# Attention and a highway layer on one core: the highway bias spread by a matrix product, in a new order of instructions

## The chip, the cores and the metric

The kernel runs on one core of a Trainium2 chip. A core has four computing engines that each run their own queue of instructions in order: PE (TensorE, matrix products, with its weight loads shown as PEld), DVE (VectorE), ACT (ScalarE) and POOL (GpSimd). A fifth queue, SP (SyncE), only issues transfers here. Engines wait for each other and for transfers by semaphores. The metric is the device time of one launch in microseconds (us); lower is better.

## What is computed

The reference first normalises queries and keys, attends, and then runs a highway layer on the heads side by side. Cut to what matters:

```python
q_n = q / (norm(q) + 1e-6);  k_n = k / (norm(k) + 1e-6)      # q, k, v: 8 x 12 x 448 x 64
scores = q_n @ k_n^T / tau                                   # tau = 0.1
attn = softmax(scores);  a = attn @ v
x = a.transpose(0, 2, 1, 3).reshape(3584, 768)
H = max(x @ w_h, 0)                                          # 768 x 768
T = sigmoid(x @ w_t + b_t)
out = T * H + (1 - T) * x
```

The change concerns b_t, the bias of the gate T, a vector of 768 numbers.

## The kernel before, in words

Work is cut into 8 batches, each of 6 pairs of heads (48 pairs, numbered s = 0 to 47), and 4 row groups of the highway layer for each batch (32 groups, g = 0 to 31). A batch has 448 rows; the first 384 lie in 3 blocks of 128 lanes, the other 64 are "tails", which two heads share.

Loading: POOL issues the large loads of q, k and v (tiles qr, kr, vr, 576 KB each, lines 342 and 365) and the two weights (wt, wh, line 372); SP issues the tails (qt, kt, vt, lines 357 to 367). All of these convert or keep the input's numbers and share the same transfer engines.

Normalising: squares (line 264 on ACT, line 258 on DVE or POOL; tile sq), folded sums (tile f, lines 421 and 425; n, line 427), a reciprocal root by Newton steps on DVE (tile rs, lines 465 to 471), and then q and k scaled into tile qn and, for the tails, kb (line 258).

Turning: for batches 0 to 3, PE turns qn and kb (lines 582, 585, 607) and DVE or ACT copies them out of PSUM (line 261). For batches 4 to 7, SP issues transposing transfers instead: qT from qn (line 572), tT from kb (line 599). The highway input xT comes from x by such transfers for batches 1 to 6 (line 757).

Attention for a pair: PE forms three blocks of scores into a ring of three PSUM tiles pS (line 642) and a block for the tail keys into a ring of two tiles pB (line 657); ACT takes the exponentials into E and Et (lines 648 and 661); PE multiplies them with the values in vp into pB again (lines 690, 694 and 710); DVE takes a reciprocal (line 718) and scales the result into x (line 720), which frees pB.

The highway group: PE multiplies xT with wt and wh into pS (lines 807, 791 for the tail groups, 779 for the last half group). ACT takes a tanh of the T half (lines 845 to 849), DVE combines (lines 867, 872, 879), DVE or POOL adds x (line 884), SP stores. For groups g below 24, b_t enters by one more matrix product of a row of ones with the bias row (tiles ones and bth). From g = 24 on (ADDED = 24), DVE adds it from tile bias instead, in which all 128 lanes hold the whole of b_t (lines 837 and 839). The two bth rows sit at lane 0 and lane 64, all other lanes of bth are zero.

PE runs its products in three forms, which the kernel calls T (two halves of 64 lanes side by side: lines 642 and 807), C (two halves of 64 columns: line 791) and F (the whole array: everything else).

The order of all of this is a table of numbers, ORDER, one number for each operation; SLOTS gives the buffer that each new tile takes in its ring; MOVED names the operations that run on their second choice of engine; URGENT lets a DVE operation wait for a POOL operation that came before it in the table. Nothing is scheduled at run time: each engine's queue is the table, filtered by engine. In the head, 40 products of the constant tile fill (line 310) keep PE running while it has nothing else.

Of the kernel before, what the change touches and what calls it, by code (L numbers as in the profile page):

```python
# [105 lines left out]
    int(n)  # L106
    for n in """
91 117 155 156 194 226 270 311 319 337 338 356 357 376 474 484 518 525 601 621 681 733 752 790 827 873 898 1059
1073 1088 1138 1175 1259 1288 1298 1338 1339 1374 1411 1428 1491 1502 1579 1596 1597 1614 1615 1617 1665 1682
""".split()  # L110
)

# [897 lines left out]
```

## Time and profile before

| What | us |
|---|---|
| Runs shown, median (lowest to highest), 3 runs | 269.06 (268.74 to 270.12) |
| Profiled execution, its span | 270.4 |
| PE busy, of that span | 244.4 |
| DVE busy | 228.5 |
| ACT busy | 206.0 |
| POOL busy | 115.9 |
| First scores of the first pair start on PE | 17.53 |
| The last product ends on PE, about | 264.4 |

For the profiled execution the span is the time on record: from its first instruction to its last. A row of the timeline has the start, the duration, the engine, the line, what is written and what is read, how often in a row, and in square brackets how long the engine was idle just before and what ended that. A row "xN" spans N instructions that follow each other. PE's busy time includes the filling and emptying of its pipeline, so a full slice does not say that PE is at its peak.

### The profile page before, as it was taken

How to read it: one execution, taken by the hardware profiler on the slowest of the kernel's cores; microseconds unless marked ns; L12 is line 12 of the kernel's file. 1: busy time of each engine (PE TensorE's matmuls, PEld its weight loads, DVE VectorE, ACT ScalarE, POOL GpSimd, SP SyncE). 2: the span in 40 equal slices, each digit the busy share in tenths (PEclk: the TensorE clock that was granted, in tenths of full speed). 3: DMA queues.
4: the chain of work that ended last, by engine and by line, in shares of the span. 5: the costliest groups of instructions: out<-in, count | busy, mean ns of one | idle time of the engine just before them, and what ended most of it. 6: DMA issues, size and time to landing. Idle time of an engine off the chain costs nothing.

```text
span 270.4 us, 9033 instructions
## 1 busy us (share of the span) xinstructions
PE 244.4 (90%) x3755; PEld 165.0 (61%) x3755; DVE 228.5 (85%) x513; ACT 206.0 (76%) x279; POOL 115.9 (43%) x151
## 2 busy tenths in 40 slices
PE   7088978999999999999899799997999999999991
PEld 3044666676776676667466557664767667767650
DVE  6599899999999898998976978997987864569894
ACT  3379999799999989989589499867868797961120
POOL 8757458563455649335450626314404522002140
PEclk9659999999999999999999799999999999999998
DMA  7999999999899797999999976999939949413133
GB/s 136 207 192 183 179 200 211 194 184 193 136 136 252 103 152 84 172 253 157 178 166 173 187 196 128 206 136 154 235 107 175 183 72 238 80 58 119 63 100 132
DMA packets 104025, 43.32 MB, mean 160 GB/s; under 512 B 97584, under 2 KB 101040, under 8 KB 103984
## 3 DMA queue, kind: packets, MB, share of 16 engines
q0 software_dynamic: 38608, 16.52, 49.1%
q1 hardware_dynamic: 63920, 25.50, 48.8%
q10 hardware_dynamic: 1456, 0.72, 1.0%
q8 instruction: 29, 0.48, 0.7%
q14 instruction: 12, 0.10, 0.1%
HBM read 38.21 MB, written 11.01 MB: 182 GB/s over the span
## 4 chain that ended last, share of the span: by engine, by line
PE 62%; DVE 20%; DMA 7%; issue 4%; ACT 3%; POOL 2%; SPq 1%; DVEq 0%; PEldq 0%; ACTq 0%; POOLq 0%
PE pS L807 26%; PE pS L642 9%; PE pB L694 8%; PE pS L791 4%; PE pB L710 4%; PE pB L657 3%; PE pB L690 3%; DMA kt<-in_k_dram 3%; DVE qn L258 3%; PE pB L582 2%; DMA qr<-in_q_dram 2%; DVE x L720 2%; DMA qT<-qn 2%; DVE f L421 2%; DVE hm L867 1%
## 5 line engine op out<-in xcount | busy, mean ns | idle before, releaser
L648 ACT ACTIVATE E<-pS 128x896 f16<-128x896 f32 x144 | 127.3, 924 | 26.2 <-PE pS L642 22.5
L807 PEld LDWEIGHTS <-xT 64*128 64x128 f16 x1128 | 53.8, 94 | 31.6 <-issue 2.6
L807 PE MATMUL pS<-wt,xT 64*128 64x384 f16 x576 | 56.6, 325 | 0.2 <-PEq L800 0.2
L807 PE MATMUL pS<-wh,xT 64*128 64x384 f16 x552 | 55.7, 323 | 0.2 <-DVE hm L867 0.2
L642 PE MATMUL pS<-qT 64*128 64x384 f16 x288 | 43.9, 332 | 2.3 <-DMA qT<-qn 1.8
L694 PE MATMUL pB<-vp,E 128*128 128x65 f16 x864 | 43.8, 194 | 0.0
L694 PEld LDWEIGHTS <-E 128*128 128x128 f16 x864 | 38.8, 98 | 2.6 <-issue 2.5
L867 DVE SCALAR_TENSOR_TENSOR hm<-pS,x 128x768 f16<-128x768 f32 (+1 forms) x33 | 27.3, 831 | 10.7 <-ACT tt L848 5.7
L642 PEld LDWEIGHTS <-qT 64*128 64x128 f16 x576 | 22.9, 95 | 19.6 <-issue 4.4
L690 PE MATMUL pB<-vp,Et 128*128 128x130 f16 x144 | 32.0, 222 | 2.3 <-DVE x L720 1.9
L258 POOL TENSOR_TENSOR qn<-kr,rs 128x384 f16<-128x384 f16 x24 | 19.8, 827 | 32.9 <-issue 10.0
L884 POOL TENSOR_TENSOR os<-x,hm 128x768 f32<-128x768 f16 (+1 forms) x11 | 15.8, 1441 | 37.7 <-DVE hm L879 17.3
L720 DVE SCALAR_TENSOR_TENSOR x<-pB,rd 128x448 f16<-128x448 f32 x48 | 29.7, 621 | 1.1
L661 ACT ACTIVATE Et<-pB 128x512 f16<-128x512 f32 x48 | 28.9, 609 | 0.9 <-PE pB L657 0.8
L642 PE MATMUL pS<-tT,qT 64*128 64x64 f16 x282 | 27.6, 190 | 0.0
L258 POOL TENSOR_TENSOR qn<-qr,rs 128x384 f16<-128x384 f16 x17 | 14.4, 850 | 14.0 <-DMA qT<-qn 5.6
L884 DVE TENSOR_TENSOR os<-x,hm 128x768 f32<-128x768 f16 (+1 forms) x22 | 18.5, 842 | 0.8 <-POOL os L884 0.6
L845 ACT ACTIVATE tt<-os 128x768 f16<-128x768 f32 (+1 forms) x8 | 6.1, 764 | 17.1 <-DVE os L839 10.0
L710 PE MATMUL pB<-vp,E 128*128 128x65 f16 x288 | 18.6, 195 | 0.5 <-POOL vp L261 0.5
L258 DVE TENSOR_TENSOR qn<-qr,rs 128x384 f16<-128x384 f16 x30 | 17.2, 577 | 0.5 <-POOL qn L258 0.4
L690 PEld LDWEIGHTS <-Et 128*128 128x128 f16 x144 | 14.1, 98 | 5.5 <-issue 4.3
L879 DVE TENSOR_TENSOR hm<-tt,hm 128x768 f16<-128x768 f16 (+1 forms) x33 | 16.4, 503 | 0.4
(116 smaller groups left out, 451.2 us busy)
## 6 DMA issues: line engine op xcount, KB each, us to landing
out_dram<-os SPq DMA_DIRECT2D x23, 384.0 KB, 3.0
vr<-in_v_dram POOLq DMA_DIRECT2D x8, 576.0 KB, 11.3
kr<-in_k_dram POOLq DMA_DIRECT2D x7, 576.0 KB, 10.8
qr<-in_q_dram POOLq DMA_DIRECT2D x7, 576.0 KB, 10.7
qt<-in_q_dram SPq DMA_DIRECT2D x16, 96.0 KB, 5.4
vt<-in_v_dram SPq DMA_DIRECT2D x16, 96.0 KB, 5.6
out_dram<-os SPq DMA_DIRECT2D x15, 96.0 KB, 2.7
kt<-in_k_dram SPq DMA_DIRECT2D x14, 96.0 KB, 6.7
```

What stands on the lines that cost most here:

```text
L258: return (nc.vector if eng == "DVE" else nc.gpsimd).tensor_mul(out_, a, c)
L642: ins = nc.tensor.matmul(dst, lhsT=qT[ln, 384 + 128 * c : 512 + 128 * c], rhs=rhs, start=True, stop=True)
L648: return nc.scalar.activation(R("E", s)[:, c, :, 0:448], R("S", 3 * s + c)[:, :, 0:448], AF.Exp, scale=inv_tau)
L661: op("ACT", f"expt {s}", lambda: nc.scalar.activation(R("Et", s)[:, 64:576], R("B", ("S", s))[:, :], AF.Exp, scale=inv_tau), key + 3, r=[( ...
L690: nc.tensor.matmul(U[:, 2 * c : 2 * c + 2, :].rearrange("p g e -> p (g e)"), lhsT=Et[:, 128 + 128 * c : 256 + 128 * c], rhs=vp[:, 6:8, :]. ...
L694: ins = nc.tensor.matmul(U[:, 2 * c + ab, :], lhsT=EF[:, j, 576 * ab + 128 * c : 576 * ab + 128 * c + 128], rhs=vp[:, 3 * ab + j, :], star ...
L710: ins = nc.tensor.matmul(U[:, 6, :], lhsT=lt, rhs=rh, start=(n == 0), stop=(n == 7))
L720: op("DVE", f"ev {s}", lambda: nc.vector.scalar_tensor_tensor(out=R("x", b)[:, :, D * p : D * p + D], in0=U_()[:, :, 0:D], scalar=0.0, in1 ...
L807: ins = nc.tensor.matmul(P[:, h, 0:MH], lhsT=lt, rhs=rh, start=(part == 0 and cc == (-1 if wi == 0 and not added else 0)), stop=(part == 1 ...
L867: return nc.vector.scalar_tensor_tensor(out=o_, in0=i0, scalar=0.0, in1=xs, op0=ALU.max, op1=ALU.subtract)
L879: op("DVE", f"gg{'h' if tail or last_ else ''} {nm}", lambda cs=cs: nc.vector.tensor_mul(R("hm", g)[:, cs], R("tt", g)[:, cs], R("hm", g)[ ...
L884: op(en, f"out{'h' if tail or last_ else ''} {nm}", lambda eng=eng, cs=cs: eng.tensor_add(R("os", g)[:, cs], xall()[:, cs], R("hm", g)[:, ...
```

## The change

Three things change. First, the transfer that spread b_t from memory over 128 lanes into tile bias goes. In its place PE multiplies a block of ones with the two bth rows, which leaves b_t in every lane of one pS tile, and DVE copies that to bias. Second, all four tables are new: ORDER, SLOTS, URGENT and MOVED. Third, by MOVED, some operations are on other engines: of the scaled q (qn from qr) DVE has 20 instead of 30 and POOL 27 instead of 17; of the last additions over 768 columns DVE has 11 instead of 15 and POOL 12 instead of 8; of the copies of v, DVE has 23 instead of 19, ACT 11 instead of 10 and POOL 14 instead of 19. All sizes, ring depths and the other operations stay.

```diff
-        op("POOL", "ld bb", lambda: nc.gpsimd.dma_start(bias[:, :], moe_b_t.partition_broadcast(128)), key + 30, w=[("bias", 0)])
+
+        def spread():
+            for h in range(2):
+                ln = slice(64 * h, 64 * h + 64)
+                ins = nc.tensor.matmul(R("S", ("bb", 0))[:, h, 0:MH], lhsT=ones[ln, 0:128], rhs=bth[ln, MH * h : MH * h + MH],
+                                       start=True, stop=True)
+            return ins
+
+        op("PE", "bbm", spread, key + 30, mode="T", r=[("zb", 0), ("bth", 0)], w=[("S", ("bb", 0))])
+        eng = pick("DVE", "ACT")
+        op(eng, "bbc", lambda eng=eng: copied(eng, bias.rearrange("p (h m) -> p h m", h=2), R("S", ("bb", 0))[:, :, 0:MH]), key + 30,
+           r=[("S", ("bb", 0))], w=[("bias", 0)])
...
-18 17 2 3 5 0 78 20 19 33 83 21 6 23 11 4 84 24 29 22 77 1 16 8 74 87 28 75 42 25 36 81 40 9 43 27 26 35 32 44
+0 28 16 3 8 39 29 18 17 12 2 43 87 79 90 9 15 27 21 1 20 40 24 26 44 25 31 33 14 73 32 85 19 22 77 23 36 5 6 45
```

The table's rows tell a reader nothing, so here is what stands in the queues at three places. Line numbers of the changed kernel are 1 lower up to line 376 and 10 higher from line 387 on.

The first place is POOL's queue where the three large loads of the last batch (7) are issued. Before, behind the fold of tile f, all three (qr, vr, kr) stand in a row:

```order
L425 TENSOR_TENSOR f_94<-f_92 128x192
L342 DMA qr_71<-in_q_dram 128x12x192
L365 DMA vr_83<-in_v_dram 128x12x192
L342 DMA kr_74<-in_k_dram 128x12x192
L258 TENSOR_TENSOR kb_81<-kt_79,rs_100 64x6x64 x2
```

In the changed kernel, POOL's queue at the same place, the loads of batch 7 from kr to vr:

```order
L435 TENSOR_TENSOR f_95<-f_93 128x192
L341 DMA kr_75<-in_k_dram 128x12x192
L260 COPY vp_87<-vr_82 128x6x64
L257 TENSOR_TENSOR qn_102<-qr_72,rs_98 128x2x3x64
L260 CAST vp_88<-vt_86 64x6x64
L341 DMA qr_72<-in_q_dram 128x12x192
L260 COPY vp_87<-vr_82 128x6x64
L364 DMA vr_83<-in_v_dram 128x12x192
```

Four operations of POOL now stand between the first and the last of the three loads.

The second place is SP's queue near there, where the key tails of batch 6 (the two loads into a kt tile) are issued. Before, both stand behind the first xT transpose of batch 3 (into xT_120) and behind two qT transposes:

```order
L757 DMA_TRANSPOSE xT_120<-x_116 128x12x128
L572 DMA_TRANSPOSE qT_106<-qn_102 128x6x128 x2
L891 DMA out_dram<-os_129 64x384
L361 DMA kt_78<-in_k_dram 64x6x64 x2
L757 DMA_TRANSPOSE xT_119<-x_116 128x9x128
```

In the changed kernel the same stretch of SP's queue; the tile of batch 6 is kt_79, and the xT transpose of batch 3 is into xT_119:

```order
L360 DMA kt_79<-in_k_dram 64x6x64
L908 DMA out_dram<-os_127 128x768
L582 DMA_TRANSPOSE qT_106<-qn_101 128x6x128
L356 DMA qt_77<-in_q_dram 64x6x64
L901 DMA out_dram<-os_130 64x384
L356 DMA qt_77<-in_q_dram 64x6x64
L767 DMA_TRANSPOSE xT_119<-x_116 128x12x128
L901 DMA out_dram<-os_130 64x384
L360 DMA kt_79<-in_k_dram 64x6x64
L582 DMA_TRANSPOSE qT_107<-qn_102 128x6x128
```

One of the two loads has moved ahead of that xT transpose, and the other has moved ahead of the two qT transposes behind it (the first of them is the last row). The square that reads these key tails has moved too: it stood in DVE's queue, and now stands in ACT's, between an exponential of a pair of batch 4 and the next.

The third place is the head. In the changed kernel's queue on PE, the new product (line 380) stands behind the last of the first 26 products of fill and in front of the turning of the first pair:

```order
L309 MATMUL pB_134<-fill 128x384
L380 LDWEIGHTS ones
L380 MATMUL pS_131<-bth,ones 128x384
L592 LDWEIGHTS qn_102
L592 MATMUL pB_134<-ident,qn_102 128x128
```

And on DVE, in the changed kernel, the copy to bias follows the copy of the first pair's turned rows (qT_107) and precedes the scaling of the next pairs:

```order
L260 COPY qT_107<-pB_134 128x896
L260 CAST bias<-pS_131 128x768
L257 TENSOR_TENSOR kb_80<-kt_79,rs_100 64x6x64
L257 TENSOR_TENSOR kb_80<-qt_77,rs_100 128x2x3x64
L257 TENSOR_TENSOR qn_101<-qr_70,rs_100 128x2x3x64
```

Before, nothing stood at either of these two spots; the transfer into bias was issued by POOL in the second half of the run. Counted over PE's whole queue, the three forms of product follow each other 135 times in a change of form before, and 162 times now: the parts of the highway products are cut finer between the scores and the products with the values.

More of the change, by code (lines that the diff above doesn't have):

```diff
@@ L93 @@
     for n in """
-001000101001011010001001001101200002010102110111002010110010120120101112011200001100210200010111101211100200011
-010121101110012010001110200001001021200211101012020101011010201110110121100211010001102011120112012121110000101
-100021101121211010022102010100101020101012011210211201110120121001020201210110020012110220201001111102111010011
-012001102000110023200021110200121101110010012110121010210102210000201001000112011010203210111001102010110021110
-201210221101220100000001111210001102221120101021010210121001021011001110121001110123101211022001101020020100112
-201101000120122101120201010102001010110220011012020001102010211111010202120100211120011122111012120012100110211
-000200021110010011001010202112221011000010120001001101210001101010221101220201130110201020012020011110100221020
-21032102101100121011102301000121210121010230201
+111001101012110000001000222020002201001101101000101101121100000012210010101110220010101211001010111101121100010
+001200110101201001001000121100112112200221101000010012101012001011001121001021201000211221110012001102001110001
+201110110011222002010002011101101112000101201012100001121111001210110010102220110222110211100010022110010111101
+210010021012023110001021100112120101002200020011210211001002000110111011021110210021122301101012101031212101111
+111010110010220201012102011011021222101110001210221031122201101121110120021021001120100101121010221020121010201
+110201211001000101222000010222102011202011201000110111110020021110021011110200111210011112210012211000100102321
+020120002010101001022010012100201011211111201112001102002010102002120021211100002011102101311102101202200100111
+002210202011102201100101230112011200212210002110
 """.replace("\n", "")
@@ L107 @@
     for n in """
-91 117 155 156 194 226 270 311 319 337 338 356 357 376 474 484 518 525 601 621 681 733 752 790 827 873 898 1059
-1073 1088 1138 1175 1259 1288 1298 1338 1339 1374 1411 1428 1491 1502 1579 1596 1597 1614 1615 1617 1665 1682
+94 195 227 271 312 339 342 357 446 475 505 524 525 587 918 958 976 994 996 1011 1119 1137 1139 1193 1196 1212
+1339 1360 1375 1376 1393 1394 1396 1411 1429 1461 1476 1492 1538 1579 1580 1597
 """.split()
```

147 rows, old and new, of tables (MOVED, ORDER) are left out of this document.

## The prediction

> **What bounds the kernel now.** I read the page first, then a table of stages, then the timeline wherever PE stood still. The page:
>
> ```profile
> span 270.4 us, 9033 instructions
> PE 244.4 (90%) x3755; PEld 165.0 (61%) x3755; DVE 228.5 (85%) x513; ACT 206.0 (76%) x279; POOL 115.9 (43%) x151
> ```
>
> PE leads, but DVE and ACT are near. The stages tell them apart (columns: window, its length, busy time and instructions of PE, PEld, DVE, ACT, POOL, then PE's clock, the transfer engines' share, GB/s):
>
> ```profile
> 17.50:50.00 32.50, 27.54 (x431) 18.88 (x431) 30.91 (x69) 31.06 (x43) 19.34 (x30) 0.98 1.37 193
> 50.00:130.00 80.00, 79.35 (x1312) 55.46 (x1310) 74.65 (x171) 73.59 (x99) 42.54 (x50) 1.00 1.17 167
> 147.00:156.00 9.00, 7.11 (x109) 4.92 (x107) 8.90 (x21) 5.19 (x7) 4.40 (x6) 0.81 1.35 180
> ...
> 186.00:190.00 4.00, 2.24 (x46) 1.51 (x41) 2.77 (x5) 2.77 (x5) 1.60 (x2) 1.00 1.13 251
> 190.00:250.00 60.00, 59.98 (x980) 41.71 (x979) 44.45 (x97) 43.87 (x59) 13.62 (x17) 1.00 0.66 138
> ```
>
> Up to 50 us DVE and ACT are full (30.91 and 31.06 of 32.50) and PE waits for them. From 50 us on PE hardly ever rests, so whatever is added to PE's own queue there lengthens the run, and whatever shortens DVE alone does not. What can be won behind 50 us are the few places where PE does stand still. The two largest:
>
> ```profile
> 136.29 1.09 POOL L342 DMA_DIRECT2D qr<-in_q_dram  x1
> ...
> 138.37 1.03 POOL L342 DMA_DIRECT2D kr<-in_k_dram  x1
> 137.63 2.21 SPq L361 DMA_DIRECT2D kt<-in_k_dram  x2
> 138.36 8.51 DMA kt<-in_k_dram
> 146.96 0.56 DVE L258 TENSOR_TENSOR sq<-kt 128x384 f16<-128x384 f32 x1 [2.31 <-DMA kt<-in_k_dram]
> 148.70 0.19 PE L657 MATMUL pB<-tT 128*128 128x64 f16 x1
> 150.78 0.22 PE L690 MATMUL pB<-vp,Et 128*128 128x130 f16 x1 [1.89 <-DVE x L720]
> 152.00:154.00 2.00, 2.00 (x34) 1.61 (x32) 1.97 (x5) 0.92 (x1) 1.56 (x3) 0.54 1.47 134
> 154.00:156.00 2.00, 2.00 (x20) 1.06 (x18) 2.00 (x5) 1.73 (x2) 1.20 (x2) 0.61 1.01 203
> ```
>
> Wait A: three large loads go out in 3 us, the key tails of batch 6 go out among them and land after 8.51 us; DVE holds 2.31 us for them, so the evictions queued behind come late, pB does not come free, and PE starts nothing from 148.70 to 150.78. It loses 2.05 us (2.08 less the 0.03 that the short product takes anyway), and soon after it resumes, from 152 us on, its clock is at 0.54 and 0.61.
>
> ```profile
> 173.74 1.08 POOL L365 DMA_DIRECT2D vr<-in_v_dram  x1
> 174.81 0.57 POOL L377 DMA_DIRECT2D bias<-in_moe_b_t_dram  x1
> DMA to landing us min/median/max: 9.2/9.2/9.2
> qT<-qn SPq DMA_TRANSPOSE x2, 6.1
> qT<-qn SPq DMA_TRANSPOSE x4, 2.8
> 186.85 0.19 PE L642 MATMUL pS<-tT,qT 64*128 64x64 f16 x2
> 188.80 0.34 PE L642 MATMUL pS<-qT 64*128 64x384 f16 x2 [1.76 <-DMA qT<-qn]
> ```
>
> Wait B: behind a vr load and the bias transfer (issued 174.81, landed 9.2 us later, 184.0), the transposes issued from 178 to 185 take 6.1 us, against 2.8 us for those from 150 to 166. PE, which needs qT, stands from 186.85 to 188.80: 1.95 us, less 0.03 for the product itself, 1.92.
>
> **The change part by part.** All terms are against the profiled execution (270.4 us); the runs' median, 269.06, lies 1.3 us below, and I apply the same difference to it.
>
> *Changes of form on PE.* These are the dearest addition: 162 instead of 135, 27 more. The price stands where the three forms follow each other without a wait:
>
> ```profile
> 248.68 1.30 PE L791 MATMUL pS<-wt,xT 128*64 128x384 f16 x14
> 249.82 1.14 PE L791 MATMUL pS<-wh,xT 128*64 128x384 f16 x12
> 250.89 0.84 PE L763 MATMUL pB<-ident,x 128*128 128x128 f16 x12
> 251.67 1.15 PE L807 MATMUL pS<-wt,xT 64*128 64x384 f16 x12
> 25.89 0.51 PE L582 MATMUL pB<-ident,qn 128*128 128x128 f16 x6
> ...
> 26.23 0.22 PE L585 MATMUL pB<-ident,kb 128*128 128x128 f16 x1
> ```
>
> Fourteen products of line 791 start in 1.14 us (249.82 less 248.68), so twelve in 0.98; but the next form starts after 1.07, 0.09 more. Six transposes take 0.34 us (26.23 less 25.89), so twelve 0.68; the next form starts after 0.78 (251.67 less 250.89), 0.10 more. With 0.10 each, 27 cost **+2.7 us** (2.4 at 0.09). PE's queue is the path from 50 us on, so nothing hides this but a wait that it falls into.
>
> *The product for the bias.* It takes one pair of 64-lane products over 384 columns, 0.16 us (a fourteenth of 1.14, times two). It stands ahead of the first pair's turning and waits for bth. Of before's two bth loads, one was issued at 4.90 among small loads and one at 22.67 behind large ones:
>
> ```profile
> 4.90 0.52 POOL L375 DMA_DIRECT2D bth<-in_moe_b_t_dram  x1 [0.22 <-DVE ones L281]
> DMA to landing us min/median/max: 5.0/13.2/21.5
> 13.91 0.29 PE L618 MATMUL pB<-ident,first_qtn 128*128 128x128 f16 x1 [7.82 <-DVE first_qtn L511]
> 12.02 0.84 ACT L264 ACTIVATE sq<-qr 128x768 f16<-128x768 f16 x1 [3.00 <-DMA qr<-in_q_dram]
> L839 DVE TENSOR_TENSOR os<-pS,bias x6: 947/956/958, 229.3 to 262.4; 128x768 f32<-128x768 f32 x6
> ```
>
> Now both go out among the first small loads, where 5.0 us is the nearest row: landed near 10 us, before PE reaches the product (its first real work was at 13.91). So no wait: **+0.16 us**. If bth came as late as 21.5 us after its issue, the first pair would wait more than 10 us; see the rivals.
>
> *The copy to bias, and the head.* The copy of 128x768 out of PSUM has no row; the nearest is the addition of the same shape, 0.956 us. It stands in DVE's queue among the second pairs' scaling, where DVE is full. Its upper bound is 0.96 us late. Against it, the first q rows are now issued ahead of a kr load that they stood behind (ACT waited 3.00 us for them, to 12.02), and turned rows of the first pair are copied by DVE instead of ACT; the lower bound is about 1.0 us early (one small load more or less in front moves a landing by about its issue time). I take **+0.3 us**, nearer the row of DVE's load, since DVE is the fuller.
>
> *The moves between engines.*
>
> ```profile
> L258 DVE TENSOR_TENSOR qn<-qr,rs 128x384 f16<-128x384 f16 x30 | 17.2, 577 | 0.5 <-POOL qn L258 0.4
> L258 POOL TENSOR_TENSOR qn<-qr,rs 128x384 f16<-128x384 f16 x17 | 14.4, 850 | 14.0 <-DMA qT<-qn 5.6 <-DVE qn L258 3.2 <-DVE os L884 2.0
> L867 DVE SCALAR_TENSOR_TENSOR hm<-pS,x 128x384 f16<-128x384 f32 x10 | 5.6, 556 | 5.8 <-ACT tt L848 5.7
> ```
>
> Ten scalings leave DVE, 10 x 0.577 = 5.8 us, and cost POOL 10 x 0.850 = 8.5 us; four of the last additions go the same way, and four copies of v and the bias copy come back to DVE. I count this as nothing: PE's queue covers it where DVE has room (44.45 of 60 us busy at the end), and POOL is busy 42.54 of 80 us. Where that cover fails, in the first 50 us, the loss is bounded by what stands in the queues: with each row at its mean duration, DVE and ACT have about 1.5 us more to do each ahead of the end of batch 3 (an estimate from the two orders), which the slower rival takes up.
>
> *The tail.* After the last product DVE now has both halves of hm ahead of the gate, so one hm more stands behind PE: between 0 and 0.56 us (the 128x384 row above, 556 ns). I take **+0.2 us**, as ACT's tanh covers part of it.
>
> *Wait A goes.* POOL's three loads are now four operations apart, one key-tail load leaves earlier and the other skips two qT transposes. Without such neighbours a kt load takes:
>
> ```profile
> kt<-in_k_dram SPq DMA_DIRECT2D x2, 96.0 KB, 2.7
> ```
>
> So the hold of 2.31 us ends, and with it 2.05 us of PE. The clock goes with it, if the wait caused its fall. At 0.54 and 0.61 over 4 us PE lost at most 0.46 x 2 + 0.39 x 2 = 1.7 us; the 20 products of the second window, 1.6 us at fourteen in 1.14, took 2.0, so 0.4 is the least. I take the middle, 1.05, as no row is nearer to either end: **-3.1 us** with the 2.05. The Trainium skill ("TensorE: Matmul & The Clock Gate", section "Why this matters for your kernels") speaks of PE-idle gaps above about 3 us as what brings the lower clock; here a stand of 2.08 us came before it. By the page this wait would cost no clock, and the sum would be 1.05 us higher.
>
> *Wait B goes.* The bias transfer is gone from in front of those transposes, and they are issued earlier against PE's use. Transposes at 2.8 us would land 3.3 us sooner than 6.1: **-1.92 us**, with 0 as the other end if vr alone delays them.
>
> Sum: 2.7 + 0.16 + 0.3 + 0.2 - 3.1 - 1.92 = -1.66 us: profiled 268.7, and on the median **267.4 us**. What is late next is PE itself, with its forms.
>
> **The rivals.** *Slower: wait A comes back on ACT* (0.24, and 0.04 for bth landing late). The square of batch 6's key tails now stands in ACT's queue between two exponentials. Counted in PE's matmuls at their rates, 6.9 us lie between the last product that the xT transpose ahead of the second kt load waits for and the last that ACT's exponential before the square waits for; it was 11.7 us on DVE. On that path stand the transpose's issue, a store's issue and the load:
>
> ```profile
> 132.30 1.40 SPq L757 DMA_TRANSPOSE xT<-x  x1
> ```
>
> 1.4 us for the first, 0.7 for the second (as between the two kt loads, 137.63 and 138.36), and the landing: with 2.7 that makes 4.8 us and holds nothing; with 8.5 it makes 10.6, ACT stands 3.7 us, pS stays full, and PE may wait as long, with 1.05 for the clock. It decides at a landing above 4.8 us. Then this place costs 4.75 us where the forecast has nothing: -1.66 + 4.75 = +3.1, 272.2 us; with the 1.5 of the first 50 us 273.7. Against it: the large loads no longer go out in one row.
>
> *No change* (0.24): wait B stays, since the vr load still stands near these transposes: -1.66 + 1.92 = +0.26, 269.3 us (0.17). Or the lower clock was not the wait's doing and comes all the same: -1.66 + 1.05 = -0.6, 268.5 us (0.07). That is where the page of the skill leads; that the fall comes so soon behind the longest stand since the head speaks against it.
>
> *Faster still* (0.10): the head gains its 1.0 instead of losing 0.3, and a third wait goes, for a tT transpose:
>
> ```profile
> 131.95 0.20 PE L657 MATMUL pB<-tT 128*128 128x64 f16 x1 [1.13 <-DMA tT<-kb]
> ```
>
> Then -1.66 - 1.3 - 1.13 = -4.1, 265.0 us. I leave this wait in the forecast, as in the changed order too that transpose is issued about as late against its use (8.1 us of products, 9.3 before).
>
> **How the numbers follow.** The forecast, both waits gone and the forms paid, has 0.38; with the case above, faster by over 0.5% (below 267.7 us; about what a measurement of this kernel can tell from no change) has 0.48, no change 0.24, slower 0.28. The range takes in both ends of these cases but for the loss of 1.5 us at the slow one, with 0.7 us for the bounds of the head and the clock below: 264.3 to 272.4 us.
>
> **What would show it.** Right: PE's rows near 140 to 160 us without a stand of 2 us and its clock at 1.00 there; transposes near 3 us before pair 36; 162 changes of form. Wrong: an ACT row that waits for kt; DVE or ACT idle for less before 50 us while PE does less there; any new stand of PE above 1 us.

## The result, and the profile after

| Kernel | median, us | runs, lowest to highest | ratio to before (95%) |
|---|---|---|---|
| before | 269.08 | 268.74 to 270.12 | |
| changed | 279.76 | 278.96 to 280.39 | 1.037 (1.031 to 1.044) |

The change costs some 10 us; the forecast was 267.4, and the range ended at 272.4. Some executions of a kernel are a few per cent longer than its fastest; the ratios here and below leave these out, so they need not be the ratio of the medians.

The page of the changed kernel: span and engines, and the group of highway products with the idle time in front of it.

```profile
span 277.6 us, 9040 instructions
PE 250.4 (90%) x3757; PEld 163.3 (59%) x3757; DVE 223.3 (80%) x508; ACT 207.9 (75%) x282; POOL 127.7 (46%) x153
L817 PE MATMUL pS<-wh,xT 64*128 64x384 f16 x552 | 59.1, 327 | 4.0 <-DMA xT<-x 3.6
```

PE now waits 3.6 us for xT in this group, which had 0.2 us of idle time in the page of before. In this profile the time is 1.84 us above the span (279.44 and 277.6), and in every run below it is 1.7 to 1.9 us above. The first profile of before, with a span of 270.4, is therefore one of an execution of about 272.2 us and not of the usual 269. So before was profiled once more (270.78 us). Stages of that second profile, columns as before (window, length, busy time and instructions of PE, PEld, DVE, ACT, POOL, then PE's clock, the transfer engines' share, GB/s):

```profile
130.00:200.00 70.00, 67.60 (x1087) 45.28 (x1085) 62.82 (x144) 56.84 (x79) 26.45 (x34) 1.00 1.10 175
200.00:260.00 60.00, 59.60 (x933) 41.21 (x929) 44.79 (x89) 38.53 (x51) 13.86 (x15) 1.00 0.54 122
```

The same stages of the changed kernel:

```profile
130.00:200.00 70.00, 63.27 (x1001) 41.30 (x999) 53.45 (x118) 53.05 (x73) 28.48 (x34) 0.98 1.11 170
200.00:260.00 60.00, 59.81 (x949) 39.44 (x945) 43.37 (x92) 42.22 (x58) 18.04 (x21) 1.00 0.54 119
```

The loss lies in one stage: from 130 to 200 us PE does 1001 products where it did 1087, and DVE 118 operations where it did 144. Behind 200 us the two run alike. The largest stand in it, from the timelines of SP, POOL and PE and the stages of 2 us:

```profile
133.04 2.24 SPq L582 DMA_TRANSPOSE qT<-qn  x1
135.32 0.61 SPq L356 DMA_DIRECT2D qt<-in_q_dram  x1
135.98 0.61 SPq L901 DMA_DIRECT2D out_dram<-os  x1
136.64 0.61 SPq L356 DMA_DIRECT2D qt<-in_q_dram  x1
137.36 1.62 SPq L767 DMA_TRANSPOSE xT<-x  x1
137.83 1.08 POOL L341 DMA_DIRECT2D kr<-in_k_dram  x1
140.04 0.19 PE L667 MATMUL pB<-tT 128*128 128x64 f16 x1
143.87 1.14 PE L817 MATMUL pS<-wh,xT 64*128 64x384 f16 x6 [3.63 <-DMA xT<-x]
144.00:146.00 2.00, 2.00 (x16) 0.94 (x14) 0.25 (x2) 0.58 (x1) 1.50 (x2) 0.50 1.44 203
```

SP issues without a pause, and the first xT transpose of batch 3 comes fifth in this row. It is issued at 137.36, half a microsecond ahead of the kr load, and lands 6.5 us later, at 143.9. PE stands for 3.7 us (3.83 less 0.03 for the product itself and 0.095 for a change of form) and then runs at a clock of 0.50. Two smaller stands follow, for the qT of pair 34 and for xT:

```profile
186.51 0.32 PE L667 MATMUL pB<-qT,tT 128*128 128x384 f16 x1 [1.08 <-DMA qT<-qn]
193.13 0.66 PE L817 MATMUL pS<-wt,xT 64*128 64x384 f16 x6 [1.03 <-DMA xT<-x]
```

In the second profile of before the stands are these: a new one for xT, then what is left of wait A, then wait B.

```profile
115.26 0.66 PE L807 MATMUL pS<-wt,xT 64*128 64x384 f16 x6 [1.76 <-DMA xT<-x]
151.06 0.22 PE L690 MATMUL pB<-vp,Et 128*128 128x130 f16 x1 [0.50 <-DVE x L720]
187.30 0.34 PE L642 MATMUL pS<-qT 64*128 64x384 f16 x2 [1.28 <-DMA qT<-qn]
```

Wait A is 0.5 us here and not 1.89, and no lower clock follows. In the profiles of three kernels below that keep before's order at this place (the product alone, more forms early, more forms late) PE loses at most 0.1 us there. So the 2.05 us of the first profile belong to that one execution.

Below, "pauses" are the time between the starts of PE's products less the products' own length and 0.095 us for each change of form; the time before the first product counts in the first row. Between the spans of the second profile and of the changed kernel lie 8.6 us:

| Where | before, again | changed | difference |
|---|---|---|---|
| forms and the bias product | | | +2.7 |
| pauses up to the first scores of pair 24 | 28.0 | 26.6 | -1.4 |
| pauses from pair 24 to pair 36 | 3.6 | 10.7 | +7.1 |
| pauses from pair 36 to the last product | 2.9 | 2.8 | -0.1 |
| behind the last product's start | 6.4 | 6.7 | +0.3 |

### The profile page after: what moved, and what is told of

The parts are those of the page before. It is cut to its first block, busy times and chain, and to the rows that moved or that the text cites. A ratio compares the mean times of both kernels' runs of the same rounds, so it can differ in the third digit from the quotient of the medians.

```text
span 277.6 us, 9040 instructions
## 1 busy us (share of the span) xinstructions
PE 250.4 (90%) x3757; PEld 163.3 (59%) x3757; DVE 223.3 (80%) x508; ACT 207.9 (75%) x282; POOL 127.7 (46%) x153
## 4 chain that ended last, share of the span: by engine, by line
PE 63%; DMA 11%; DVE 11%; ACT 8%; SPq 3%; issue 2%; DVEq 0%; PEldq 0%
PE pS L817 28%; PE pS L652 9%; PE pB L704 7%; DMA qT<-qn 5%; PE pS L801 5%; ACT E L658 5%; PE pB L720 4%; PE pB L667 3%; PE pB L700 3%; DMA kt<-in_k_dram 3%; PE pB L592 3%; DMA xT<-x 2%; ACT Et L671 2%; DVE hm L877 1%; DMA first<-in_q_dram 1%
## 5 line engine op out<-in xcount | busy, mean ns | idle before, releaser
L817 PEld LDWEIGHTS <-xT 64*128 64x128 f16 x1128 | 49.9, 95 | 38.6 <-DMA xT<-x 5.2
L817 PE MATMUL pS<-wh,xT 64*128 64x384 f16 x552 | 59.1, 327 | 4.0 <-DMA xT<-x 3.6
L817 PE MATMUL pS<-wt,xT 64*128 64x384 f16 x576 | 60.9, 324 | 1.2 <-DMA xT<-x 1.0
L652 PE MATMUL pS<-qT 64*128 64x384 f16 x288 | 45.6, 332 | 3.7 <-DVE qT L260 1.6
L894 POOL TENSOR_TENSOR os<-x,hm 128x768 f32<-128x768 f16 (+1 forms) x15 | 22.6, 1508 | 55.8 <-DVE hm L889 27.9
L257 POOL TENSOR_TENSOR qn<-qr,rs 128x384 f16<-128x384 f16 x27 | 24.0, 893 | 27.1 <-DMA qT<-qn 14.7
L257 POOL TENSOR_TENSOR qn<-kr,rs 128x384 f16<-128x384 f16 x25 | 21.6, 868 | 30.4 <-DVE rs L480 7.1
L728 DVE RECIPROCAL rd<-pB 128x7 f32<-128x7 f32 x48 | 9.2, 197 | 12.1 <-PE pB L704 6.9
L431 DVE TENSOR_TENSOR f<-sq 128x1152 f16<-128x1152 f16 (+1 forms) x21 | 14.6, 700 | 2.5 <-POOL f L435 2.3
L859 ACT ACTIVATE tt<-pS 128x768 f16<-128x768 f32 x18 | 14.7, 816 | 1.9 <-PE pS L817 1.5
```

The costliest lines, as they stand in the source:

```text
L257: return (nc.vector if eng == "DVE" else nc.gpsimd).tensor_mul(out_, a, c)
L652: ins = nc.tensor.matmul(dst, lhsT=qT[ln, 384 + 128 * c : 512 + 128 * c], rhs=rhs, start=True, stop=True)
L817: ins = nc.tensor.matmul(P[:, h, 0:MH], lhsT=lt, rhs=rh, start=(part == 0 and cc == (-1 if wi == 0 and not added else 0)), stop=(part == 1 ...
L859: return nc.scalar.activation(T.rearrange("p (h m) -> p h m", h=2), P[:, :, 0:MH], AF.Tanh, scale=0.5)
L894: op(en, f"out{'h' if tail or last_ else ''} {nm}", lambda eng=eng, cs=cs: eng.tensor_add(R("os", g)[:, cs], xall()[:, cs], R("hm", g)[:, ...
```

## The experiments

Lines of the kernels below lie a few numbers off those shown, as their tables have other lengths. Each ratio is to runs of before on the same chip, whose medians went from 270.25 to 271.59 us. A profile shows one execution, and it can lie far from the kernel's median: 283.17 against 279.63 us (batch 7 later), 285.68 against 283.67 (the tables alone), 269.01 against 272.42 (qr of batch 6 later).

**Before, once more.** 270.78 us, told above.

> The kernel before, unchanged, profiled once more. In the profile of the changed kernel the span is 1.84 us below its own time (277.6 and 279.44 us); in the first profile of before it is 270.4 us, which is above the median of the runs. Theory 1: that first profile shows an execution longer than the usual one, and waits A and B, or one of them, are not in the usual run; then this span is about 267.2 us and one or both of the stands (2.05 and 1.92 us) are absent. Theory 2: the waits are in every run; then both stands come again within 0.5 us and the span is 269 to 271 us.

Each theory held in part: the span is 269.0 us, as by theory 2, and wait B is in both profiles (1.92 and 1.45 us), but wait A shrank from 2.05 to 0.66 us (0.50 of idle in its row), and a stand of 1.93 us for xT is new. Thirteen runs of before on this chip spread from 267.86 to 273.78 us, and its two profiles differ in which transfer PE loses most to.

**The two halves of the change.** Product alone, in before's order:

```diff
-POOL  bias<-in_moe_b_t_dram (behind vr of batch 6)
+POOL  second bth row behind the first
+PE    bias product ahead of the first pair's turning
+DVE   copy to bias behind the scaling of the first q tails
```

> Before's order and engines, with the bias spread by the product and copied by DVE, and no transfer into bias. Theory 1 (the new tables alone lose the time): within 1 us of before, 268 to 270 us, or 267.2 if wait B was in before's usual run and goes with the transfer. Theory 2 (the product or its copy delays the head, which is the loss): 272 us or more, with the first scores on PE later than 17.5 us by as much.

Measured 271.02 us, ratio 1.001 (0.997 to 1.006). The tables alone, with the transfer:

```diff
-PE    bias product
-DVE   copy to bias
+POOL  bias<-in_moe_b_t_dram (fourth operation behind vr of batch 6)
```

> The changed kernel's order and engines, with the bias spread by the transfer again (issued by POOL right behind the vr load of batch 6, as before) and without the product and its copy. Theory 1 (the new tables lose the time): 278 to 281 us, with the stand of PE near 140 us and the lower clock behind it (3.7 and 1.6 us) in place. Theory 2 (product and copy in the head are the loss): 272 us or less.

Measured 283.67 us, 1.042 (1.031 to 1.053). The transfer did not go out right behind the vr load, as expected: three operations of POOL stood between, and it was issued at 190.49 us, 14 us after that load. The stand near 140 us is there all the same, before it. The product costs nothing that can be measured, and without it the new order is no better. The loss is the tables' own.

**The stand at 140 us: SP's order.** A first try put the transpose ahead of the last scalings of x, too. There the last two of batch 3's six pairs are not in what it turns, and DVE waits for it, so it says little:

```diff
 SP
+xT of batch 3, first
 qT, qt, store, qt
-xT of batch 3, first
```

> The changed kernel with one move: on SP, the first xT transpose of batch 3 stands ahead of one qT transpose, two qt loads and one store that it stood behind. Theory 1 (PE's stand of 3.7 us near 140 us comes from the late issue at 137.36): the transpose is issued near 135, the stand shrinks by 2 us or more, and the lower clock behind it (1.6 us) shortens with it: 275 to 277.5 us. Theory 2 (the landing of 6.5 us under the kr load and the stores is the cause): the landing grows as the issue comes earlier, and the time stays at 279 to 280 us.

Measured 280.04 us, 1.037 (1.030 to 1.044); DVE held its scaling 5.2 us for the transpose. The second try keeps the scalings ahead:

```diff
 SP
-qT 27, qt, store, qt, xT of batch 3 first
+qt, qt, xT of batch 3 first, qT 27, store
```

> The changed kernel, its SP queue alone reordered at one place: the two qt loads of batch 6, then the first xT transpose of batch 3, then the qT transpose and the store that stood ahead of it. All it needs is scaled before it is issued. Theory 1 (PE's stand near 140 us is a transpose issued at the same moment as the kr load): issue near 135, 2 to 3 us ahead of the kr load, landing in 4.5 us or less, the stand below 0.6 us and the clock behind it at 1.00: 274 to 276 us. Theory 2 (another wait stands right behind, so that the time only moves): the stand comes back within 15 us at another row and the time is 278 us or more.

Measured 280.25 us, 1.032 (1.024 to 1.041). The transpose was issued at 136.2 and landed in 4.1 us, and PE stood at the same place all the same, now for the qT of pair 27 that had given up its turn. This one now went out half a microsecond ahead of the kr load (at 138.0; kr at 138.5) and landed in 5.4:

```profile
140.19 0.20 PE L671 MATMUL pB<-tT 128*128 128x64 f16 x1
143.39 0.32 PE L671 MATMUL pB<-qT,tT 128*128 128x384 f16 x1 [3.00 <-DMA qT<-qn]
```

Theory 2 was right here: the stand only moved to another row. The transpose that comes second on SP is both issued later and beside the load, so this run does not tell the two causes apart.

**The stand at 140 us: the kr load.**

```diff
 POOL
-kr of batch 7, vp, qn, vp, qr of batch 7
+vp, qn, vp, kr of batch 7, qr of batch 7
```

> The changed kernel with one move on POOL: the kr load of batch 7 stands three operations later, right ahead of the qr load, so that it goes out about 2 us after the xT transpose and not 0.5 us after it. Theory 1 (the load's neighbourhood makes the transpose land late): the transpose is issued near 137.4 as before and lands in about 4.3 us, not 6.5; the stand near 140 is 1.3 to 1.8 us: 276 to 278 us. Theory 2 (the late place on SP is the whole cause): landing 6 us or more and 279 to 280.5 us.

Measured 277.17 us, 1.023 (1.016 to 1.031). The xT transpose lands in 3.9 us and the stand at 140 is gone, so its neighbour was the cause of the 6.5, as theory 1 said. Then PE stands for the second xT of batch 3, which takes SP 4.51 us to issue and lands 13.4 us after its start:

```profile
143.69 4.51 SPq L771 DMA_TRANSPOSE xT<-x  x1
157.09 0.66 PE L821 MATMUL pS<-wt,xT 64*128 64x384 f16 x6 [2.28 <-DMA xT<-x]
```

**Are the loads of batch 7 the cause?** The same cut in both kernels takes most of their bytes away:

```diff
-dma_start(R(rname, b)[:, :, :], main_src(src, b))
+n = 1 if b == 7 else 12      # q, k and v alike
+dma_start(R(rname, b)[:, 0:n, :], main_src(src, b)[:, 0:n, :])
```

> The changed kernel with the three large loads of batch 7 cut to one head of twelve (48 KB each and not 576); the other heads of batch 7 are computed from what the tiles held before, so only its time is read. All instructions, waits and places stay. Theory 1 (the new order stands because its transposes go out beside these loads): no stand of PE above 1 us between 130 and 175 us, 272 to 274.5 us, and 3 to 4.5 us above the kernel before cut in the same way (27 changes of form are 2.6 of it). Theory 2 (the new order's chain from pair to pair is too tight in itself): stands stay in 130 to 175 us, and 276 us or more.

> The kernel before with the same three loads cut to one head of twelve, its time alone to be read. Theory 1: before's transposes hardly meet these loads, so it gains 1 to 2 us at most, 268.5 to 270 us. Theory 2 (the loads cost every order the same): it gains as much as the changed kernel does, 4 us or more, 267 us or less.

Changed kernel: 274.78 us, 1.012 (1.008 to 1.016). Before: 268.91 us, 0.990 (0.986 to 0.993). Without these bytes the changed kernel gains 2.6% of before's time, some 6.9 us (1.037 to 1.012), and before 1.0%, some 2.8. Their stages from 130 us, changed kernel first:

```profile
130.00:200.00 70.00, 65.73 (x1051) 43.37 (x1049) 58.34 (x126) 56.79 (x79) 29.03 (x36) 1.00 0.87 154
```

```profile
130.00:200.00 70.00, 68.95 (x1110) 46.23 (x1107) 63.78 (x147) 58.38 (x81) 25.47 (x35) 1.00 0.88 158
```

The changed kernel was 86 products behind here (1087 less 1001); without the bytes it does 50 more (1051), and before 23 more (1110). So the loads explain some 4 us of the 10 (6.9 less 2.8, each from runs on different chips), and neither theory has all of it: the changed kernel still stands, for xT at 142 and, beside the vr load of batch 6 that was left whole, for qT at 183.

```profile
142.28 0.66 PE L821 MATMUL pS<-wh,xT 64*128 64x384 f16 x6 [1.38 <-DMA xT<-x]
183.09 0.32 PE L671 MATMUL pB<-qT,tT 128*128 128x384 f16 x1 [2.06 <-DMA qT<-qn]
```

**Can the loads be put elsewhere?** Four runs moved them in the changed kernel (places on POOL, with the times at which they went out):

```diff
-kr 137.8, qr 140.6, vr 144.8
+kr 150.9, qr 155.2, vr 159.1     # batch 7 later
+kr 150.0, qr 154.4, vr 158.2     # later and first (and SP as in the second try)
+kr 140.2, qr 152.7, vr 167.0     # apart
+kr 139.5, qr 150.0, vr 154.3     # spaced
```

> The changed kernel with the three large loads of batch 7 later in POOL's queue: kr behind the scaling of a q block of pair 30 (issue near 156 us instead of 137.8), qr near 160 instead of 140.6, vr near 163 instead of 144.8; their first readers come after 170 us. Theory 1 (the transposes of batches 3 and 4 land late because these loads move beside them): the second xT transpose of batch 3 (13.2 us) and the qT ones near 142 (8.8 to 9.5) land in 5 us or less, no stand of PE above 1 us is left between 135 and 160, and the time is 272 to 275 us. Theory 2 (the transposes jam each other, whatever is loaded): the landings stay above 8 us, and the time is 277 us or more.

> Both mends in the changed kernel: the loads of batch 7 later on POOL, and on SP the first xT transpose of batch 3 ahead of a qT transpose and a store. Theory 1 (what is left against before is 27 changes of form, 2.6 us, the product, and the head): 271 to 273.5 us, no stand above 1 us from 130 to 165. Theory 2 (the new order lacks room elsewhere): 275 us or more, with stands at rows that had none.

> The changed kernel with the loads of batch 7 whole, but apart from each other: kr three operations later (as in an earlier run), qr behind the scaling of a q block of pair 30 (near 152 us), vr behind one of k of pair 34 (near 168 us). Theory 1 (it is several large loads at once that make a transpose land late): transposes between 137 and 170 us land in 6 us or less, each stand below 1.5 us, 273 to 276 us. Theory 2 (one load beside it is enough, and the stands only move): a stand above 2 us somewhere from 150 to 180 and 277 us or more.

> The changed kernel with the loads of batch 7 whole and about 7 us apart: kr near 140, qr near 152.7, vr behind the scaling of a k block of pair 31 (near 158), so that vr is out of the way of the vr load of batch 6 (near 170). Theory 1 (the new order can be mended by where its loads stand): with each landing in 7 to 9 us, no two of them overlap for long; transposes land in 7 us or less, stands between 130 and 175 us sum to 3 us or less (10.7 from pair 24 to 36 in the changed kernel, pauses of all kinds counted), 274 to 276 us. Theory 2 (this order has no place where a load hurts nothing): a stand of 2 us or more, 277 us or more.

Measured 279.63 (1.033; 1.027 to 1.038), 280.39 (1.034; 1.029 to 1.040), 282.58 (1.042; 1.037 to 1.047) and 283.91 us (1.048; 1.043 to 1.053). Landings of four transposes, and PE's pauses from pair 24 to pair 36, all in us:

| Kernel | xT batch 3, first | second | tT batch 5 | xT batch 4, first | pauses |
|---|---|---|---|---|---|
| before, again | 3.9 | 10.9 | 4.4 | 4.0 | 3.6 |
| changed | 6.5 | 13.2 | 3.9 | 4.5 | 10.7 |
| batch 7 later | 3.8 | 3.7 | 8.6 | 3.8 | 14.4 |
| later and first | 4.0 | 3.7 | 11.4 | 3.8 | 13.5 |
| apart | 3.9 | 7.3 | 3.7 | 11.4 | 13.4 |
| spaced | 3.7 | 7.4 | 13.0 | 3.7 | 15.7 |
| changed, batch 7 small | 4.5 | 4.6 | 2.9 | 3.7 | 6.3 |
| before, batch 7 small | 3.9 | 5.6 | 2.8 | 4.2 | 2.6 |

As to landings theory 1 held each time: where the loads went away, 13.2 us became 3.7. As to the time theory 2 held each time: the next transpose met them. The spaced run shows it best, although the loads did not come out 7 us apart as planned, but 10.5 and 4.3; vr goes out 0.64 us ahead of the tT transpose, SP then needs 9.92 us to issue three qT, and PE stands 8 us:

```profile
154.28 1.07 POOL L368 DMA_DIRECT2D vr<-in_v_dram  x1
154.92 3.01 SPq L613 DMA_TRANSPOSE tT<-kb  x1
159.47 9.92 SPq L586 DMA_TRANSPOSE qT<-qn  x3
167.96 0.24 PE L671 MATMUL pB<-tT 128*128 128x64 f16 x1 [8.05 <-DMA tT<-kb]
```

In the run with loads apart the last load met another load instead, vr of batch 6, and xT of batch 4 landed after 11.4 us:

```profile
166.96 1.07 POOL L368 DMA_DIRECT2D vr<-in_v_dram  x1
169.62 1.07 POOL L368 DMA_DIRECT2D vr<-in_v_dram  x1
181.59 0.82 PE L821 MATMUL pS<-wt,xT 64*128 64x384 f16 x4 [7.62 <-DMA xT<-x]
```

**The late place alone, put into before.**

```diff
 SP
-xT of batch 3 first, qT 29, qT 28, store, kt
+qT 29, qT 28, store, kt, xT of batch 3 first
```

> Before's kernel with one move on SP: the first xT transpose of batch 3 stands behind two qT transposes, a store and a kt load that it stood ahead of, so that it is issued near 138 us, beside the three loads of batch 7, as in the changed kernel, and not near 133. Theory 1 (this place alone makes the changed kernel's stand): landing 6.5 to 11 us, a stand of PE of 3 us or more near 141 and the lower clock behind it; 273 to 276 us. Theory 2 (something else of the new order makes it): landing below 5 us and 269 to 271 us.

Measured 272.97 us, 1.007 (1.003 to 1.012). The stand is there, the slow landing is not (4.0 us):

```profile
141.06 1.15 PE L811 MATMUL pS<-wt,xT 64*128 64x384 f16 x12 [2.71 <-DMA xT<-x]
```

A late issue alone makes a stand of 2.9 us, of which 2 us are left at the end. At 140 us in the changed kernel both causes are at work, the place on SP and the load beside it: in five runs with the load moved or small this transpose landed in 3.7 to 4.5 us, and of the stand of 3.7 us there stayed 1.2 to 1.5 in three (batch 7 later, apart, small) and 0.4 or less in two (kr later, spaced).

**The price of a form.** Twice 14 moves in before's PE queue, 28 changes of form more:

```diff
 PE
-F F | T T
+F T F T
```

> Before's kernel with 14 products or parts of products moved by at most two places in PE's queue, between pairs 9 and 17, so that PE changes its form 163 times and not 135; nothing else moves. Theory 1 (0.095 us for each change of form, and PE's queue is the path there): from the first scores of pair 9 to those of pair 18 it takes 2.4 to 2.9 us longer than in the kernel before (44.0 us), and the time is before plus 2.7. Theory 2 (the price hides behind other engines in this stage): the stage grows by less than 1 us.

> Before's kernel with 14 products moved by at most two places in PE's queue, all from pair 34 on, so that PE changes its form 163 times and not 135; nothing else moves. There DVE and ACT are busy for 44 of 60 us and PE hardly ever stands, so the price of a form is seen alone. Theory 1 (0.095 us each, nothing hides it): from the first scores of pair 33 to the last product 2.4 to 2.9 us longer than in the second profile of before (88.3 us there, with a stand of 1.45 us in it), and the time 2 to 3 us above before. Theory 2 (less than half of that): below 1.3 us.

Early: 278.85 us, 1.021 (1.009 to 1.033); from pair 9 to pair 18 (the first of the three blocks of scores as the kernel numbers them) it takes 48.8 us, not 43.9, and three short stands that the moves brought (0.35, 0.56 and 0.40) are in it. That is more than either theory had. Late: 276.18 us, 1.017 (1.015 to 1.019). There the stretch from pair 33 to the last product takes 91.9 us, not 88.3: 3.6 more. Apart from two that both kernels have at the end, its stands above 0.25 us (0.34, 0.75, 0.50, 0.28, 0.55) sum to 2.4 and those of before (1.45, 0.27) to 1.7, so 0.7 of it is stands and 2.9 is 28 forms: 0.10 each. The bare price is as forecast; in place a moved product costs more, as short stands come with it. The whole is 4.6 us above before, as this run also stands 2.3 us for xT of batch 2, with the lower clock behind it, where nothing was moved.

**A better version?** Before's order with the product, and its qr load of batch 6 no longer beside xT of batch 2; then two loads of batch 7 later as well.

```diff
 POOL
-qr of batch 6, kb
+kb, qr of batch 6
```

> Before's order with the product for the bias, as in the run of the product alone, and one more move: POOL issues the qr load of batch 6 behind the scaling of kb, about 6 us later, so that it no longer goes out within 1 us of the first xT transpose of batch 2 (landing 7.6 us there, PE's stand 1.7 us, then the clock at 0.50). Theory 1: that transpose lands in 4.5 us or less, stand and lower clock go, and no new one comes: 2 to 4 us below the product alone, 267 to 269 us. Theory 2 (the squares of the late load hold DVE): the stand of PE moves behind 120 us and the time stays at 270 to 272.

> Before's order with the product for the bias and three large loads later on POOL: qr of batch 6 behind the scaling of kb, and of batch 7 kr behind the scaling of kb of batch 5 (near 147 us), vr behind a scaling of pair 32 (near 159); qr of batch 7 stays. Theory 1 (PE's stands come from transposes beside large loads, and most of them can be had back): stands of PE behind 100 us sum to less than 1.5 us (4.5 in the second profile of before), 266 to 268 us. Theory 2 (the stands move to the places where the loads go now): sum 3 us or more and 269 to 271 us.

First: 272.42 us (268.33 to 275.07), 0.998 (0.992 to 1.004), no measurable gain, although in the profile xT of batch 2 landed in 4.4 us, not 7.6, and its stand went. Second: 275.49 us, 1.018 (1.013 to 1.023): the loads met qT and tT near 150 to 165 (5.5 to 8.9 us), with stands of 2.1 and 1.4. Neither is faster than before.

## Why the prediction was wrong

- **Changes of form, +2.7:** right (2.9 for 28 in the late run).
- **The product, +0.16, and the tail, +0.2:** small, as forecast. The product took 0.44 us at PE's lower clock in the head; the tail 0.3.
- **The head, +0.3:** too low. First scores start at 15.3 us, not 17.5, but at pair 18 PE's pauses are 25.6 us against 24.6: +1.0. Between pairs 18 and 24 before loses more than that again, with its stand for xT.
- **Wait A goes, -3.1:** the step that failed first. It was priced from one execution, some 2 to 3 us longer than the usual one; in the second profile of before it is worth 0.7 us and no clock.
- **Wait B goes, -1.92:** its place, the scores of pair 36, has no stand in the changed kernel, but the qT of pair 34 and an xT 7 us later cost 1.24 and 1.20 us. In the changed kernel the term was a shift and no gain. In before's order part of it is real: with the product alone PE loses 0.5 us at this place and not 1.45 (one profile each). The working has a slip, too: 6.1 us is the median of two transposes, and the one that PE waited for took 4.8:

```profile
183.97 4.78 DMA qT<-qn
```

- **The first xT transpose of batch 3, put at nothing:** the step that cost most. Under wait A the prediction followed the key-tail loads ("one key-tail load leaves earlier"), and its slower rival counted this transpose only as 1.4 us of issue ahead of such a load. Its own landing and the products that read it got no term. But it now stood fifth in a row that SP issues without a pause, beside the kr load that the spreading of POOL's loads had put there; the queue's rows showed this place. It cost 3.7 us and the lower clock behind it. Counted in PE's work from the last product that its x waits for, it had 6.2 us of room, 7.4 before. Waits A and B together were to bring 5.0 us; against the second profile of before, the pauses from pair 24 to pair 36, where both lie, grew by 7.1.
- **The rivals:** the slower one looked for a late transfer at the right place, but at the wrong one of them. Its kt load did land after 7.7 us, above the 4.8 from which it was to decide, and ACT waited 1.85 us for it at 148.2; PE lost 0.7 there, not 3.7.

Shown is that the tables alone lose the time, that most of it lies between pairs 24 and 36, that the transposes of batches 3 to 5 beside these loads often land in 6.5 to 13 us, and in 6 or less where the loads are cut or gone, and that loads of batch 7 cost the new order some 4 us more than the old one. Only argued is why before's order bears them better: SP issues no transpose from 143 to 150 us there, while they move. No run put such a gap into the changed kernel. Room before the reader counts as well: before's second xT transpose of batch 3 lands after 10.9 us in its second profile, and PE does not stand for it, as it reads it 13.3 us after the issue. Nor did a run part the new order from the new engines of some operations. About 6 us of the difference stay without those loads; 2.7 are forms, and some 3.7 are pauses from pair 24 to pair 36 (6.3 against 2.6), the largest of them waits for xT and qT.

## What to carry to other kernels

A stand found in one profile is worth what a second profile still shows of it. When a table moves transfers, list for each transpose its place on its issuing queue, the large loads issued within a few microseconds of it, and the work left until its first reader; compare that room with the slow landing, not the usual one. Moving a load away from one late transfer pays only if a gap without transfers is left for it.

## What the runs showed of the hardware

A transpose of this kernel lands in 2.7 to 5.7 us with no large load near, and in up to 13.4 us beside one, though not each time (4.0 us in the run with the late place). Over all nineteen traces, behind 100 us: of 488 transposes with no load of 576 KB in flight, 2 took more than 6 us, both beside the bias transfer of the run of the tables alone (6.2 and 7.3 us); of 234 with such a load in flight, 110 did. The issue of such a transpose can hold SP, too: 3.01 and 4.51 us in rows above, where 1.62 is the row of a quicker one, so that everything behind it on SP is late. The Trainium skill ("DMA: Bandwidth & Descriptors", section "Rules for kernel authors") says that all issuers run on the same 16 engines and that a transpose next to ordinary transfers needs nothing. It says this of waiting for each other's completion, to keep the data right; no row here speaks against that, but in time the neighbour costs what is told above.

PE's clock can fall after stands well below 3 us, and not after each of the same length. Product alone, behind a stand of 1.71 us, then before's second profile, behind one of 1.93:

```profile
116.00:118.00 2.00, 2.00 (x16) 0.50 1.23 294
```

```profile
116.00:118.00 2.00, 2.00 (x32) 1.00 1.25 279
```

In the first of these, two shorter stands of 0.37 and 0.38 us lay within 4 us ahead. The Trainium skill ("TensorE: Matmul & The Clock Gate", section "What's actually happening") tells of a free-running window of 3413 ns; that a stand's position, not its length alone, decides agrees with these rows. The clock records of the traces show the window: up to the last product every stretch at 0.50 lasts 3.41 us or a multiple, and within a run all of them lie on one grid of 3.41 us. Laid on that grid, the nineteen traces have 1220 windows at full clock from 26 to 250 us. Count as idle the time between the starts of PE's products less the products' own length: the 15 windows that the lower clock follows hold at least 2.16 us of it, the 1205 others at most 2.10. So in this kernel the clock falls when PE is idle for some 2.1 us or more of one window. The stand of 1.71 us falls with other idle time into one window (2.16 in all); that of 1.93 is split over two (1.22 and 1.54). Wait A of the first profile fell whole into one (2.20), and wait B with 2.10 just missed.
